# Score matmuls of the first head pair: from 64 contracted rows to 128, through query tiles padded with zeros

## The chip, the cores and the metric

One Trainium2 chip, one core of it. The time is device microseconds (us) of one execution; lower is better. The kernel before takes 513.86 us, the median of three runs that lie between 513.81 and 513.95 us.

## The reference, cut to what matters

The program is attention, then a feed-forward network, then a mixture of experts. The change lies in the attention scores; what follows uses them.

```python
B, H, S, D = q.shape                       # 2, 8, 576, 64
scores = scale * np.matmul(q, k.transpose(0, 1, 3, 2))
mask = block_i >= block_j                  # blocks of 64 positions
scores = np.where(mask, scores, -1000000000.0)
scores = scores - np.max(scores, axis=-1, keepdims=True)
attn = np.exp(scores)
attn = attn / (np.sum(attn, axis=-1, keepdims=True) + 1e-09)
return np.matmul(attn, v)
...
x = attn_out, tokens by model width: 1152 x 512
h = x @ w_in; g = elu(h); x = g @ w_out    # feed-forward, 2048 wide
...                                        # router to 8 experts, two layers each, scaled by the gate
```

## The kernel before, in words

Sixteen heads (two batches of eight) are worked on as eight pairs of heads; a pair is called m, its heads a and b. `part1` does the attention, `part2` the feed-forward network and the router, `part3` the experts. On all five engines of `part1` the order of the work is the program's own, written out by hand in the string `ORDER` (lines 26 to 34): each word is a step, the letter a or b is the head, the last digit says how many rounds behind the round i the step's pair is. A round is one pass through `ORDER`.

The steps that matter here:

- `K` (`turn`, line 358) transposes a pair's keys or queries on TensorE, 128 positions at a time, so that the 64 head dimensions of head a lie in rows 0 to 63 and those of head b in rows 64 to 127. `k` then splits the result in a high part (ScalarE, line 375) and a low part, the rest (VectorE, line 376). Keys and queries are each done in two groups g, of 256 and 320 positions.
- `S` (`scores`, line 396) multiplies queries by keys into PSUM. A head's 576 queries are five tiles t (one of 64 and four of 128), handled in three parts; a piece is one tile against at most 512 keys. The first tile of a round's scores is `S20`. Each piece has one bank in PSUM, and the next head's piece may only start when the exponentials of the one before it have been read out.
- A product in full precision is high*high + high*low + low*high. For the pairs 1 to 7 the queries' high and low parts are stacked in one tile of 128 rows (`stack`, line 342, four DMAs on SP's queue) and the keys' high part is doubled (`double`, line 331, on GpSimd), so that two matmuls of 128 rows do the work: `kk` against `qq`, and the keys' low part `kl`, with zeros in the other head's rows (`lows`, line 352), against `qq`. Pair 0 is not stacked: it takes three matmuls per piece of 64 rows each, on the rows of the head (line 411). Its output has `nq` rows (line 406), which is 64 for the first tile.
- The last 64 columns of a tile's scores are masked by a small matmul of 128 rows (line 425).
- `M` takes the row maxima on VectorE (line 436), `E` the exponentials on ScalarE (line 449), `D` sums and reciprocals on VectorE, `N` the normalization on GpSimd (line 476), `T` the transposes of the probabilities on TensorE (lines 495, 499 and 520), `V` the product with the values (line 536).

Before round 0 the program fills constants. VectorE's memsets come first: `kr` and `qr` (line 554), then `mrow` and `mcol` (lines 562 to 564). GpSimd fills the larger tiles meanwhile (lines 566 to 578). TensorE runs 42 small matmuls on `mrow` (line 581), transposes pair 0's keys and queries (lines 582 to 585), and runs four more small matmuls (line 588). Twelve more stand ahead of the eighth to the nineteenth of the steps `S`, `T` and `K` (line 643).

Of the kernel before, what the change touches and what calls it, by code (L numbers as in the profile page):

```python
# [9 lines left out]
FP32 = mybir.dt.float32  # L10
F32R = mybir.dt.float32r
# [3 lines left out]
ACTF = mybir.ActivationFunctionType  # L15
ALU = mybir.AluOpType
# [26 lines left out]
def attention_ffn_moe(  # L43
# [13 lines left out]
    nc = tc.nc  # L57
    B, H, S, D = q.shape
# [216 lines left out]
    def part1():  # L275
# [5 lines left out]
        xx_p = p1.enter_context(tc.tile_pool(name="xx", side="left", bufs=2))  # L281
# [15 lines left out]
        qraw, kraw, vt, qT, kT, prob, stat = {}, {}, {}, {}, {}, {}, {}  # L297
# [6 lines left out]
        )  # L304
        PROB = [[at.tile([128, 640], FP32, name=f"prob{part}{i}") for i in range(2)] for part in range(3)]

        KLO = [xx_p.tile([128, 2, S], F32R, name=f"kl{i}", bufs=1) for i in range(2)]

        def load(m, src, ring, queue=nc.sync):
# [42 lines left out]
        def lows(m):  # L352

            for h in range(2):
                own = slice(64 * h, 64 * h + 64)
                nc.sync.dma_start(out=KLO[m % 2][own, h].bitcast(FP32), in_=kT[m][1][own].bitcast(FP32))

        def turn(m, which, g, pool=ps_t, tag="t"):

            src, dst, sc = (qraw, qT, SCALE) if which == "q" else (kraw, kT, 1.0)  # L360
            if g == 0:
                dst[m] = tuple(qt_p.tile([128, S], F32R, tag=which + x, name=which + x) for x in "hl")
            js = range(NK)[2 * g:2 + (NK - 2) * g]
            a, e = 128 * js[0], min(S, 128 * (js[-1] + 1))
            bank = pool.tile([128, 512], FP32, tag=tag, name="qkT")
            ps = bank[:, 0:e - a]
            for j in reversed(js):
                nc.tensor.transpose(
                    out=bank[:, 128 * j - a:128 * j - a + 128],
                    in_=src[m][:, j].rearrange("r h d -> r (h d)"),  # L370
                    identity=ident,
                )
            hv, lv = (x[:, a:e] for x in dst[m])
            return [
                lambda: nc.scalar.activation(out=hv, in_=ps, func=ACTF.Copy, scale=sc),
                lambda: nc.vector.scalar_tensor_tensor(
                    out=lv, in0=ps, scalar=sc, in1=hv.bitcast(FP32), op0=ALU.mult, op1=ALU.subtract
                ),
            ]


        parts = [[(4, 0)], [(3, 0), (0, 448)], [(2, 0), (1, 320)]]
# [1 line left out]
        def split(t):  # L384

            nk = sum(QT[t])
            nb = (nk + 511) // 512
            return nb, nk // nb
# [7 lines left out]
        def scores(n, part, i):  # L396

            m, h = divmod(n, 2)
            r0 = 64 * h
            t, b, c0, k0, w = PIECES[part][i]  # L400
            if c0 == 0:
                banks[n, part, b] = ps_s.tile([128, 512], FP32, tag=f"s{part}{b}", name="s")
            bank, (q0, nq) = banks[n, part, b], QT[t]
            rows = slice(r0, r0 + 64)

            wq = 128 if m else nq
            if m:
                xq = stacked[m, "q"][:, h]
                todo = [(xq, stacked[m, "k"][:, h]), (xq, KLO[m % 2][:, h])]
            else:  # L410
                todo = [(qT[m][x][rows], kT[m][z][rows]) for x, z in ((0, 0), (0, 1), (1, 0))]
            end = t > 0 and k0 + w == q0 + nq
            for y, (x, z) in enumerate(todo):
                nc.tensor.matmul(
                    out=bank[0:wq, c0:c0 + w],
                    lhsT=x[:, q0:q0 + wq],
                    rhs=z[:, k0:k0 + w],
                    start=(y == 0 and (part != 2 or c0 == 0)),
                    stop=(y == len(todo) - 1 and not end),
                    skip_group_check=(part == 2),  # L420
                )

            def mask():
                if end:
                    nc.tensor.matmul(  # L425
                        out=bank[:, c0 + w - 64:c0 + w],
                        lhsT=mrow, rhs=mcol, start=False, stop=True,
                        skip_group_check=(part == 2),
                    )

            return mask
# [130 lines left out]
        nc.vector.memset(mrow, 0.0)  # L562
        nc.vector.memset(mrow[:, 0:64], 1.0)
        nc.vector.memset(mcol, -1e8)
        stats = [[st_p.tile([128, 8], FP32, name=f"stat{i}{j}") for j in range(3)] for i in range(3)]
        for x in stats:
            nc.gpsimd.memset(x[1], 1.0)
# [3 lines left out]
        for x in VT:  # L571
            nc.gpsimd.memset(x[64:128, NK - 1], 0.0)
        for x in KLO:
            for h in range(2):
# [7 lines left out]
        for w in "kq":  # L582
            for g in range(2):
                for f in turn(0, w, g, ps_s, ("s10", "s20", "s00", "s01")[2 * "kq".index(w) + g]):
                    f()
# [32 lines left out]
        def do(name, h, m):  # L618
# [25 lines left out]
            if kind == "S":  # L644
                pend[n, name] = scores(n, *rest)
                if name == "S21":
                    pend[n, "S20"]()
                if name != "S20":
                    pend[n, name]()
            elif kind == "M":  # L650
                largest_of_two(n, 4) if rest == [0, 2] else largest(n, *rest)
            elif kind == "E":
                power(n, *rest)
            elif kind == "D":
                if rest == [0, 0]:
                    total_of_two(n, 4)
                elif rest[1] == (1 if rest[0] == 0 else 0):
                    total(n, rest[0])
                else:
                    inverse(n, rest[0])  # L660
            elif kind == "N":
                norm(n, *rest)
            elif kind == "T":
                pend[n, name] = turn_ends(n) if name == "TE" else turn_p(n, rest[0])
            elif kind == "t":
                pend[n, name[:2].upper()][rest[-1]]()
            elif kind == "K":
                if m + 1 < NM:
                    pend[n, name] = turn(m + 1, "kq"[h], rest[0])
            elif kind == "k":  # L670
                if m + 1 < NM:
                    pend[n, name[:2].upper()][rest[1]]()
# [629 lines left out]
    with tc.manual_schedule(engines=every):  # L1302
        part1()
# [31 lines left out]
```

## Time and profile before

| what | value |
|---|---|
| median of the runs | 513.86 us (513.81 to 513.95) |
| the profiled execution | 514.5 us, its span from first to last instruction 512.8 us |
| TensorE (PE) busy | 487.3 us, 95% of the span, 2842 matmuls |
| VectorE (DVE) busy | 341.3 us, 67% |
| ScalarE (ACT) busy | 311.7 us, 61% |
| GpSimd (POOL) busy | 118.0 us, 23% |
| mean granted TensorE clock | 0.976 of full speed |

The profile is one execution on the chip. PE is TensorE's matmuls, PEld its weight loads, which run beside them; SPq, ACTq and the like are the engines' queues, which issue DMAs. A clock of 1.00 is TensorE's upper level, 2.4 GHz; 0.50 is the lower, 1.2 GHz. Times in the rows are us from the span's start, durations us unless marked ns. A matmul's end is modelled, so durations of neighbours overlap; the distance between two starts is the better measure of what a matmul costs in a stream. The stretches:

| us from the start | what runs |
|---|---|
| 0 to 9.6 | constants, pair 0's keys and queries |
| 9.6 to 24.3 | pair 0's scores, both heads |
| 24.3 to about 112 | the remaining pairs, a round of some 11.7 us each |
| about 112 to 440 | feed-forward network, router, first experts |
| 440 to 512.8 | last experts |

### The profile page before, as it was taken

How to read it: one execution, taken by the hardware profiler on the slowest of the kernel's cores; microseconds unless marked ns; L12 is line 12 of the kernel's file. 1: busy time of each engine (PE TensorE's matmuls, PEld its weight loads, DVE VectorE, ACT ScalarE, POOL GpSimd, SP SyncE). 2: the span in 40 equal slices, each digit the busy share in tenths (PEclk: the TensorE clock that was granted, in tenths of full speed). 3: DMA queues.
4: the chain of work that ended last, by engine and by line, in shares of the span. 5: the costliest groups of instructions: out<-in, count | busy, mean ns of one | idle time of the engine just before them, and what ended most of it. 6: DMA issues, size and time to landing. Idle time of an engine off the chain costs nothing. (4 is left out here: it accounts for less than half of the span.)

```text
span 512.8 us, 8712 instructions
## 1 busy us (share of the span) xinstructions
PE 487.3 (95%) x2842; PEld 403.3 (79%) x2842; DVE 341.3 (67%) x828; ACT 311.7 (61%) x699; POOL 118.0 (23%) x219
## 2 busy tenths in 40 slices
PE   7999999999999999999999999989898889999994
PEld 6678888879997889999998888767676768786683
DVE  4489898969977999994464365564467965461451
ACT  4478899867865666753554455373567875552551
POOL 6266878650000000000000022311121330100211
PEclk9599999999999999999999999999999989999998
DMA  8758775503689985340131043269389886280100
GB/s 195 164 140 197 186 167 133 153 15 117 185 249 228 281 272 159 97 138 12 35 91 42 1 143 124 67 242 336 117 324 345 296 273 267 80 317 20 42 33 24
DMA packets 61254, 80.86 MB, mean 158 GB/s; under 512 B 33170, under 2 KB 33170, under 8 KB 61200
## 3 DMA queue, kind: packets, MB, share of 16 engines
q1 hardware_dynamic: 58368, 75.18, 48.4%
q0 software_dynamic: 1632, 4.72, 2.5%
q8 instruction: 28, 0.46, 0.4%
q10 hardware_dynamic: 1200, 0.30, 0.3%
q14 instruction: 26, 0.21, 0.1%
HBM read 62.17 MB, written 12.41 MB: 145 GB/s over the span
## 5 line engine op out<-in xcount | busy, mean ns | idle before, releaser
L260 PE MATMUL acc<-wbh,gh 128*128 128x512 f32 x144 | 57.3, 398 | 0.0
L260 PE MATMUL acc<-wbh,gl 128*128 128x512 f32 x144 | 57.2, 397 | 0.0
L260 PE MATMUL acc<-wbl,gh 128*128 128x512 f32 x144 | 57.1, 397 | 0.0
L904 POOL DMA_INDIRECT disp<-y_all,slot x9 | 9.1, 1016 | 201.7 <-DVE e L245 179.0
L87 DVE TENSOR_TENSOR xl<-rb,xh 128x1024 fp32r<-128x1024 f32 (+1 forms) x36 | 38.9, 1100 | 22.2 <-ACT xh L1116 19.0
L476 POOL TENSOR_SCALAR prob<-prob,stat 128x576 f32<-128x576 f32 (+3 forms) x80 | 42.3, 542 | 32.5 <-DVE stat L470 19.4
L449 ACT ACTIVATE prob<-s,stat 128x288 f32<-128x288 f32 (+4 forms) x96 | 45.4, 480 | 2.4 <-DVE stat L464 1.1
L243 ACT ACTIVATE e<-h 128x384 f32<-128x384 f32 x48 | 23.3, 484 | 36.4 <-PE h L233 34.0
L186 DVE SCALAR_TENSOR_TENSOR cv_t<-r,cv_t 128x512 int32<-128x512 int32 x64 | 44.1, 690 | 0.3
L87 DVE TENSOR_TENSOR xl<-ra,xh 128x1024 fp32r<-128x1024 f32 (+1 forms) x36 | 39.3, 1101 | 7.0 <-ACT xh L1116 6.1
L233 PE MATMUL h<-xh,wah 128*128 128x384 f32 x192 | 42.3, 341 | 1.6 <-DVE e L245 1.4
L436 DVE TENSOR_REDUCE stat<-s 128x1 f32<-128x288 f32 (+4 forms) x96 | 37.8, 423 | 6.5 <-PE s L425 4.3
L233 PE MATMUL h<-xl,wah 128*128 128x384 f32 x192 | 41.6, 337 | 0.0
L233 PE MATMUL h<-xh,wal 128*128 128x384 f32 x192 | 41.1, 336 | 0.0
L245 DVE SCALAR_TENSOR_TENSOR e<-e,h 128x384 f32<-128x384 f32 x48 | 26.4, 550 | 21.2 <-ACT e L244 21.0
L233 PEld LDWEIGHTS h<-xh,wah 128*128 128x128 f32 x192 | 34.2, 188 | 6.8 <-DVE e L245 2.9
L1216 PE MATMUL acc<-xh,gh 128*128 128x512 f32 (+1 forms) x96 | 39.3, 410 | 0.0
L1216 PE MATMUL acc<-xh,gl 128*128 128x512 f32 (+1 forms) x96 | 38.0, 395 | 0.0
L1216 PE MATMUL acc<-xl,gh 128*128 128x512 f32 (+1 forms) x96 | 37.8, 394 | 0.0
L1243 POOL DMA_INDIRECT out<-o,gt x12 | 11.7, 972 | 112.0 <-ACTq L1290 34.6
L1116 ACT ACTIVATE xh<-ra 128x1024 fp32r<-128x1024 f32 (+1 forms) x36 | 34.3, 961 | 5.0 <-PE h L233 2.8
L249 ACT ACTIVATE gh<-e 128x384 fp32r<-128x384 f32 x48 | 25.1, 522 | 16.7 <-DVE e L245 16.1
(171 smaller groups left out, 1178.5 us busy)
## 6 DMA issues: line engine op xcount, KB each, us to landing
ra<-in_moe_w SPq DMA_DIRECT2D x32, 512.0 KB, 6.1
rb<-in_moe_w SPq DMA_DIRECT2D x32, 512.0 KB, 7.9
r<-in_moe_w_in SPq DMA_DIRECT2D x16, 512.0 KB, 6.4
r<-in_moe_w_out SPq DMA_DIRECT2D x16, 512.0 KB, 4.4
disp<-z SPq DMA_DIRECT2D x18, 257.0 KB, 6.9
rows<-disp SPq DMA_DIRECT2D x14, 257.0 KB, 4.3
out<-z SPq DMA_DIRECT2D x9, 256.0 KB, 4.0
kr<-in_k SPq DMA_DIRECT2D x16, 128.0 KB, 2.9
```

What stands on the lines that cost most here:

```text
L87: eng.tensor_tensor(out=lo, in0=x, in1=hi.bitcast(FP32), op=ALU.subtract)
L186: nc.vector.scalar_tensor_tensor(out=st["t"], in0=x(), scalar=scalar, in1=st["t"], op0=op, op1=ALU.bitwise_or)
L233: nc.tensor.matmul(out=h[:, f, :], lhsT=w[:, kk, (f0 + f) * 128:(f0 + f + 1) * 128], rhs=x[:, kk, t0:t0 + n], start=(i == 0), stop=(i == l ...
L243: nc.scalar.activation(out=e, in_=hf, func=ACTF.Relu, scale=-1.0)
L245: nc.vector.scalar_tensor_tensor(out=e, in0=e, scalar=-1.0, in1=hf, op0=ALU.add, op1=ALU.max)
L249: nc.scalar.activation(out=gh, in_=ef, func=ACTF.Copy)
L260: nc.tensor.matmul(out=acc[t], lhsT=x[:, f, t * 128:(t + 1) * 128], rhs=w[:, f0 + f, :], start=(first and f == 0 and i == 0), stop=(last a ...
L436: nc.vector.tensor_reduce(out=stat[n][0][0:nq, t + b:t + b + 1], in_=banks[n, part, b][0:nq, c0:c0 + w], axis=AX.X, op=ALU.max, negate=True,)
L449: nc.scalar.activation(out=prob[n, part][0:nq, c0 + k0:c0 + k0 + w], in_=banks[n, part, b][0:nq, c0:c0 + w], func=ACTF.Exp, bias=stat[n][0 ...
L476: nc.gpsimd.tensor_scalar(out=p, in0=p, scalar1=stat[n][2][0:nq, t:t + 1], scalar2=0.0, op0=ALU.mult, op1=ALU.add)
L1116: lambda: nc.scalar.activation(out=hi, in_=r, func=ACTF.Copy),
L1216: nc.tensor.matmul(out=acc[0:n], lhsT=x[:, f % 4, 0:n], rhs=y[:, f % 2, :], start=(f == 0 and i == 0), stop=(f == NF - 1 and i == 2),)
```

## The change

Two tiles `QZ` of 128 rows, 2 heads and 576 positions are added, one for the high and one for the low part of pair 0's scaled queries. Each head's slot holds that head's 64 rows and zeros in the other 64; four memsets on VectorE write the zeros, placed behind all its other constants. Pair 0's queries are split from PSUM into these tiles, a head at a time, so that each of the two groups takes two ScalarE and two VectorE instructions on 64 rows where it took one and one on 128. Pair 0's score matmuls then contract 128 rows: the padded queries against the keys of both heads. Their number stays three per piece. The output of the first tile's piece takes 128 rows in place of 64.

```diff
+        QZ = [xx_p.tile([128, 2, S], F32R, name=f"qz{i}", bufs=1) for i in range(2)]
...
-            hv, lv = (x[:, a:e] for x in dst[m])
-            return [
-                lambda: nc.scalar.activation(out=hv, in_=ps, func=ACTF.Copy, scale=sc),
-                lambda: nc.vector.scalar_tensor_tensor(
-                    out=lv, in0=ps, scalar=sc, in1=hv.bitcast(FP32), op0=ALU.mult, op1=ALU.subtract
-                ),
-            ]
+            def split(hv, lv, x):
+                return [
+                    lambda: nc.scalar.activation(out=hv, in_=x, func=ACTF.Copy, scale=sc),
+                    lambda: nc.vector.scalar_tensor_tensor(
+                        out=lv, in0=x, scalar=sc, in1=hv.bitcast(FP32), op0=ALU.mult, op1=ALU.subtract
+                    ),
+                ]
+            if m == 0 and which == "q":
+                res = []
+                for h in range(2):
+                    own = slice(64 * h, 64 * h + 64)
+                    res.append(split(*(x[own, h, a:e] for x in QZ), ps[own]))
+                return [f for fs in zip(*res) for f in fs]
+            return split(*(x[:, a:e] for x in dst[m]), ps)
...
-            wq = 128 if m else nq
+            wq = 128
...
-                todo = [(qT[m][x][rows], kT[m][z][rows]) for x, z in ((0, 0), (0, 1), (1, 0))]
+                todo = [(QZ[x][:, h], kT[m][z]) for x, z in ((0, 0), (0, 1), (1, 0))]
...
         nc.vector.memset(mcol, -1e8)
+        for x in QZ:
+            for h in range(2):
+                nc.vector.memset(x[64 - 64 * h:128 - 64 * h, h].bitcast(FP32), 0.0)
```

## Rows read from the trace of the kernel before

**Rows 1.** Windows by stage: length, busy us (instructions) per engine, clock, DMA share, GB/s

```profile
9.60:13.30 3.70, 3.70 (x24) 2.82 (x23) 2.39 (x7) 2.07 (x6) 2.13 (x4) 1.00 1.03 234
13.30:25.10 11.80, 11.45 (x50) 7.79 (x49) 4.95 (x21) 5.57 (x22) 3.15 (x6) 0.50 0.71 158
...
37.40:49.10 11.70, 11.70 (x107) 9.43 (x106) 10.47 (x41) 10.42 (x37) 8.09 (x14) 1.00 0.80 197
```

**Rows 2.** Windows of 0.2 us, PE alone: length, busy us, clock, DMA share, GB/s

```profile
13.20:13.40 0.20, 0.20 (x3) 0.85 0.28 63
...
26.80:27.00 0.20, 0.20 (x2) 0.52 0.73 229
```

**Rows 3.** Timeline of PE, rounds 0 and 1: start, us, instruction, idle before it

```profile
17.07 0.74 PE L414 MATMUL s<-kh,qh 64*128 64x448 f32 x1
...
21.69 0.23 PE L425 MATMUL s<-mcol,mrow 128*128 128x64 bf16 x1
...
24.34 0.45 PE L495 MATMUL pT<-ident,prob 128*128 128x128 f32 x1 [0.19 <-DVE stat L470]
...
25.08 0.62 PE L414 MATMUL s<-kk,qq 128*128 128x320 f32 x1
...
27.37 0.66 PE L520 MATMUL pE<-ident,prob 128*128 128x128 f32 x4
```

**Rows 4.** Waits of PE from 36 to 442 us, the longest single one: total us, times, longest

```profile
PE hx L1195 <- DVE dl L87: 2.3, 1, 2.3
```

**Rows 5.** Windows of 2 us among the experts, PE alone: length, busy us, clock, DMA share, GB/s

```profile
402.00:404.00 2.00, 0.94 (x7) 1.00 0.93 278
...
416.00:418.00 2.00, 2.00 (x6) 0.53 0.34 68
```

**Rows 6.** Timeline of DVE: its first memsets, and the splits of pairs 0 and 1

```profile
0.91 0.30 DVE L554 MEMSET kr<- 64x128 f32 x2 [0.91 <-PEq L1320]
...
7.28 0.87 DVE L376 SCALAR_TENSOR_TENSOR kl<-qkT,kh 128x256 fp32r<-128x256 f32 x2 [5.35 <-ACT kh L375]
8.07 0.81 DVE L376 SCALAR_TENSOR_TENSOR ql<-qkT,qh 128x256 fp32r<-128x256 f32 x2
8.80 0.81 DVE L376 SCALAR_TENSOR_TENSOR kl<-qkT,kh 128x256 fp32r<-128x256 f32 x2
```

**Rows 7.** Timeline of PE ahead of the first scores

```profile
9.27 0.44 PE L368 MATMUL qkT<-ident,qr 128*128 128x128 f32 x2 [0.79 <-DVE kl L376]
```

**Rows 8.** Timeline of PE: scores of pair 0, head a

```profile
9.63 0.41 PE L414 MATMUL s<-kh,qh 64*128 64x320 f32 x1
...
11.55 0.20 PE L425 MATMUL s<-mcol,mrow 128*128 128x64 bf16 x1
...
11.68 0.24 PE L414 MATMUL s<-kh,qh 64*64 64x64 f32 x1
...
13.57 0.29 PE L643 MATMUL warm<-mrow 128*128 128x128 bf16 x1
```

**Rows 9.** Timeline of PE: in round 2, the steps of 24.34 to 27.37 us

```profile
37.39 0.27 PE L495 MATMUL pT<-ident,prob 128*128 128x128 f32 x1
...
38.88 0.20 PE L425 MATMUL s<-mcol,mrow 128*128 128x64 bf16 x1
38.92 0.28 PE L414 MATMUL s<-kk,qq 128*128 128x64 f32 x1
...
39.15 0.66 PE L520 MATMUL pE<-ident,prob 128*128 128x128 f32 x4
```

**Rows 10.** Timeline of ACT: the split and exponentials ahead of head b's second part

```profile
14.54 0.44 ACT L375 ACTIVATE qh<-qkT 128x320 fp32r<-128x320 f32 x1 [1.79 <-PE qkT L368]
...
15.77 0.49 ACT L449 ACTIVATE prob<-s,stat 128x288 f32<-128x288 f32 x1
```

**Rows 11.** SP's queue: head a's second stacking DMA; median us to landing of such

```profile
15.56 0.54 SPq L348 DMA_DIRECT2D qq<-ql x1
...
qq<-ql SPq DMA_DIRECT2D x14, 144.0 KB, 2.5
```

More of the change, by code (lines that the diff above doesn't have):

```diff
@@ L398, in scores @@
             m, h = divmod(n, 2)
-            r0 = 64 * h
             t, b, c0, k0, w = PIECES[part][i]
@@ L403, in scores @@
             bank, (q0, nq) = banks[n, part, b], QT[t]
-            rows = slice(r0, r0 + 64)
-            wq = 128 if m else nq
+            wq = 128
             if m:
```

## The prediction

> **What bounds the kernel now.** TensorE is busy for 95% of the span, so I look for stretches where it works below its pace. I read the windows by stage first. From 9.6 to 13.3 us PE works without a gap at the upper clock; from 13.3 to 25.1 us it is still busy for 11.45 of 11.80 us, but the granted clock is 0.50, the 1.2 GHz level; in round 2 it is at 1.00 again and never idle [rows 1]. The small windows put the fall between 13.2 and 13.4 us and the return at 27.0 us [rows 2]. The timeline says what PE did before each. Ahead of the fall it had run 64-row score matmuls since 9.63 us, with 128-row work only in short masks and warming matmuls between [rows 8]. The clock stayed low through head b, also 64 rows. At 24.34 us 128-row transposes start, at 25.08 us the first 128-row scores, and 1.9 us after those the clock is back [rows 3]. All through the low stretch VectorE (4.95 of 11.80 us) and ScalarE (5.57) have room [rows 1], so there PE sets the pace.
>
> Where time won here ends up: from round 2 PE is the bound, 11.70 busy us in 11.70 [rows 1], and the order of work is fixed, so a round that begins earlier moves everything behind it. Later waits of PE are on engines that move along with it; the longest single one, 2.3 us on VectorE [rows 4], is between two stages of the same chain. I expect a gain at round 2 to reach the end whole, but for the clock among the experts (below).
>
> **The change, part by part.** *Memsets.* Four on VectorE, each 64x576. The nearest row is `kr`: two of 64x128 in 0.30 us, 0.15 us each [rows 6]. Scaled by 576/128 that is 0.68 us each, 2.7 us in all; by count alone 0.6 us. I take the upper end. VectorE sits idle for 5.35 us before its first split at 7.28 us [rows 6], and the memsets stand behind `mrow`, on which PE's warming matmuls wait, so they cost nothing; if they took over 5.35 us, what is over would delay the splits.
>
> *The split by heads.* Each of the two query groups takes two VectorE instructions where it took one, so two more. Two of 128 rows took 0.73 us from start to start (8.07 to 8.80) [rows 6]. For 64 rows the same length bounds it above, half of that below, 0.37 us more; with as many elements per row I take the same length: +0.73, say 0.8. Behind it stands pair 1's key split, for whose buffer PE waits 0.79 us before the transposes at 9.27 us [rows 7]; so the first score starts at 10.4 us in place of 9.63. ScalarE's two more instructions run beside these.
>
> *Head a's scores.* The number and the columns of the matmuls stay; wider output of the first tile adds nothing to the columns. What goes is the change between 64-row and 128-row matmuls at every mask and warming matmul. From a mask to the next score it is 0.13 us with 64-row scores (11.55 to 11.68) [rows 8] and 0.04 us where both have 128 rows (38.88 to 38.92) [rows 9]: 0.09 us for a change. From 9.63 to 13.57 us there are nine of them: -0.8 us. The bounds are 0 and 1.0. So head a ends where it did, at 13.57 us.
>
> *The clock, head b.* With 128-row scores I expect no fall. From 13.57 to 17.07 us PE does three transposes and head b's first part at the lower clock; half of 3.50 us is 1.75, which puts the second part at 15.3 us. Its bank is free only when ScalarE has split pair 1's queries and read out head a's first two exponentials of that part, 1.23 us (14.54 to 15.77) [rows 10], from about 14.05 us, so also at 15.3: no further gain there. From 17.07 us [rows 3] to the last mask at 21.69 is 4.62 us, half of it 2.31; seven row changes less take off 0.6 (0 to 0.6): 17.0 us. From that mask to 24.34 us VectorE's maxima and splits set the pace, 2.65 us; I take 2.5 us (between 2.3, the part without waits on PE, and 2.65). The transposes of round 1 then start at 19.5 us in place of 24.34: 4.8 us earlier.
>
> *Round 1 up to 27.37 us.* The stretch takes 3.03 us, mostly at the lower clock [rows 3]; the same steps in round 2 take 1.76 us (37.39 to 39.15) [rows 9]. That is 1.27 us more, if GpSimd's normalization keeps up; 0 if it does not.
>
> *Queues.* SP's stacking DMAs for pair 1 wait on the same split and move little. Head a's second is issued at 15.56 us and such a one lands 2.5 us later [rows 11], 18.1 us, ahead of the 19.9 us at which it is now wanted: covered by 1.8 us. Behind them SP only issues loads, which are wanted a round later. The unused query tile of pair 0 costs nothing.
>
> **Sum:** +0.8 - 0.8 - 1.8 - 2.9 - 0.1 - 1.3 = -6.1 us. The profiled execution took 514.5 us with a span of 512.8 us, 0.6 us over the median; the difference is taken off the median: 513.86 - 6.1 = **507.8 us**. Bounds of this case: without the row changes of head b, the 0.15 us and the last term, a gain of 4.1 us, 509.8 us. On the other side round 1 still holds PE idle time: PE was never idle in round 2 [rows 1], and if round 1 came to the same, some 1 us more is won, 506.8 us.
>
> One thing moves either way. Among the experts PE has gaps, and not all are followed by the same clock: at 402 us, where PE is busy for only 0.94 of 2 us, it stays at 1.00, while at 416 us it is at 0.53 over two busy us [rows 5]. Which of them cost the clock may differ once everything lies 6 us earlier. A stretch like that costs about 1.5 us, won or lost; I take none.
>
> **The rivals.** *A, forecast:* no fall, 506.8 to 509.8 us, likeliest 507.8.
>
> *B, a short fall.* PE's gap before the first scores doubles, from 0.79 to about 1.6 us, and the clock falls there, ahead of the first score; 128-row scores then bring it back. The nearest rows are 1.9 us from the first such scores to the return, and 3.7 us of scores before the fall [rows 2, 3, 8]. At half pace that gives back 0.9 to 1.9 us: 508.7 to 509.7, or 511 with A's lower bound. Against it: the clock stayed up at 402 us [rows 5].
>
> *C, rows are not the cause.* The clock falls and returns as before, because it hangs on something that the padding leaves alone. The Trainium skill, "TensorE: Matmul & The Clock Gate", Part 1, says that the gate follows how busy TensorE has recently been, with no word of how many rows a matmul fills; by that the padding would leave the clock as it is. What is left in this case is +0.8 for the splits, -0.8 and -0.6 for the row changes: 513.3 us, between 512.5 (splits free) and 514.7 (no row changes gained). Against it speaks the row in which PE is busy for 11.45 of 11.80 us at the lower clock [rows 1]: that page's rule alone does not explain it, and what differs on its two sides is the rows. For it: the zeros may count as little as the missing rows did. But the later pairs' `kl` has zeros in half its rows too, and their clock is 1.00.
>
> *D, slower.* The doubled gap lowers the clock before the first score, and rows of zeros do not bring it back until round 1. Head a's 3.1 us then take 6.2: its end moves from 13.57 to 16.6 us, +3.0, less 0.6 for head b: 516.3 us. It decides once the gap over 0.79 us is enough for a fall; without a fall ahead of the scores there is no way to such a loss.
>
> **How the numbers follow.** A 0.70, B 0.12, C 0.10, D 0.08. The time is A's. Its own range is 506.8 to 509.8; B's reaches to 511. The range goes from 506.4, which allows for a part of a low stretch among the experts that is won, to B's 511.0 us; C and D, 0.18, lie outside. About 0.2%, 1.0 us, is what a measurement of this kernel can tell from no change. A and B are faster: 0.82. C is within it: 0.10. D is slower: 0.08.
>
> **What would show it.** Right: a granted clock of 1.00 from 9.6 to 27 us, the first score near 10.4 us, head b's second part waiting shortly for ScalarE near 15.3 us, round 1's transposes near 19.5 us, round 2's near 31.3 us, rounds of 11.7 us after. A clock of 0.50 from about 13.3 us with 128-row matmuls shows C, one that is low from about 10 us B or D, told apart by its return. First scores still at 9.6 us would prove the split's term wrong; a gain at round 2 that is not there at the end would prove the passing on wrong.

## The result, and the profile after

The changed kernel took 507.33 us, the median of 12 runs, against 513.78 us for the kernel before in 12 runs beside them: a ratio of 0.989, 95% interval 0.987 to 0.991. Forecast were 507.8 us and a range of 506.4 to 511.0. The single runs lie between 505.8 and 512.3 us, before between 511.2 and 515.5: both kernels vary by several us, more than the three runs shown ahead of the prediction suggested. Line numbers shift by up to 12 in the changed kernel.

The windows by stage of the changed kernel, to be read against [rows 1] (columns as there):

```profile
9.60:13.30 3.70, 3.21 (x25) 2.83 (x25) 2.82 (x8) 1.97 (x6) 2.46 (x4) 1.00 1.09 249
13.30:25.10 11.80, 10.24 (x86) 8.62 (x85) 9.24 (x39) 9.26 (x35) 5.92 (x12) 1.00 0.71 159
25.10:27.00 1.90, 1.90 (x17) 1.59 (x15) 1.90 (x7) 1.20 (x5) 1.77 (x3) 1.00 0.90 301
37.40:49.10 11.70, 11.70 (x107) 9.45 (x106) 10.98 (x45) 10.56 (x38) 8.32 (x15) 1.00 0.87 216
```

From 13.3 to 25.1 us the clock is at 1.00 in place of 0.50, and PE gets through 86 matmuls in place of 50. The low stretch is gone, and the later rounds are unchanged, 11.70 us busy in 11.70.

The timeline of PE shows where the stages begin, to be read against [rows 3, 8 and 9]:

```profile
5.80 0.72 PE L370 MATMUL qkT<-ident,kr 128*128 128x128 f32 x5
...
7.13 0.71 PE L370 MATMUL qkT<-ident,kr 128*128 128x128 f32 x5
10.09 0.44 PE L370 MATMUL qkT<-ident,qr 128*128 128x128 f32 x2 [2.25 <-DVE kl L379]
10.29 0.39 PE L423 MATMUL s<-kh,qz 128*128 128x320 f32 x1
...
13.36 0.22 PE L655 MATMUL warm<-mrow 128*128 128x128 bf16 x1
...
15.33 0.48 PE L423 MATMUL s<-kh,qz 128*128 128x448 f32 x1 [0.29 <-ACT prob L458]
...
17.53 0.20 PE L434 MATMUL s<-mcol,mrow 128*128 128x64 bf16 x1
...
19.72 0.30 PE L504 MATMUL pT<-ident,prob 128*128 128x128 f32 x1 [0.25 <-DVE stat L479]
...
21.50 0.66 PE L529 MATMUL pE<-ident,prob 128*128 128x128 f32 x4
...
31.57 0.27 PE L504 MATMUL pT<-ident,prob 128*128 128x128 f32 x1
```

Round 2 begins at 31.57 us where it began at 37.39, 5.8 us earlier. The first score begins 0.7 us later (10.29 against 9.63), behind a wait for VectorE that has grown from 0.79 to 2.25 us [rows 7]. This although the first transposes start at 5.80 us here and at 6.37 us in the profile of before; over the profiles of this study, with the same front of the program or not, that start lies between 5.78 and 6.37 us, so it is chance.

The feed-forward network's first accumulation then starts at 114.18 us against 120.02, again 5.8 us earlier. The span is 504.7 us against 512.8, 8.1 us less; the other 2.3 us come from later places that differ between executions of the same program (last section).

### The profile page after: what moved, and what is told of

Read it like the earlier page. It is cut to its first block, busy times and chain, and to the rows that moved or that the text cites. A ratio compares the mean times of both kernels' runs of the same rounds, so it can differ in the third digit from the quotient of the medians.

```text
span 504.7 us, 8722 instructions
## 1 busy us (share of the span) xinstructions
PE 479.9 (95%) x2842; PEld 400.2 (79%) x2842; DVE 344.2 (68%) x834; ACT 311.9 (62%) x701; POOL 118.9 (24%) x219
## 5 line engine op out<-in xcount | busy, mean ns | idle before, releaser
L249 ACT ACTIVATE gh<-e 128x384 fp32r<-128x384 f32 x48 | 25.1, 523 | 16.6 <-DVE e L245 16.0
```

Of the source, the lines that this page charges most:

```text
L249: nc.scalar.activation(out=gh, in_=ef, func=ACTF.Copy)
```

## The experiments

Because the end varies, I compare by marks in round 0 to 2, which the order of work fixes. All are us from the start of one profiled execution; "low" is the stretch at a clock of 0.50. "First transposes" are those of pair 0's keys, "pair 1's keys" the last group of transposes ahead of PE's wait for VectorE.

| kernel | first transposes | pair 1's keys | first score | low | head b's second part | round 1 | round 2 |
|---|---|---|---|---|---|---|---|
| before | 6.37 | 7.76 | 9.63 | 13.3 to 27.0 | 17.07 | 24.34 | 37.39 |
| changed | 5.80 | 7.13 | 10.29 | none | 15.33 | 19.72 | 31.57 |
| changed, again (e8) | 6.37 | 8.46 | 11.65 | 11.3 to 14.8 | 18.13 | 22.50 | 34.35 |
| changed, third (e12) | 6.37 | 8.11 | 11.27 | none | 16.31 | 20.68 | 32.54 |
| e1, own 64 rows | 6.36 | 8.04 | 11.38 | 13.9 to 31.0 | 19.87 | 27.46 | 40.85 |
| e2, before with 128 rows | 6.37 | 8.27 | 9.95 | none | 14.84 | 19.04 | 30.91 |
| e3, head a on 64 | 5.91 | 7.23 | 10.56 | 12.2 to 19.0 | 18.87 | 23.31 | 35.16 |
| e4, no warming | 5.84 | 7.16 | 10.32 | none | 15.17 | 19.32 | 31.20 |
| e5, memsets twice | 5.78 | 7.10 | 10.72 | 11.9 to 15.3 | 17.34 | 21.71 | 33.58 |
| e6, head b's split later | 5.89 | 7.22 | 8.91 | none | 14.34 | 18.72 | 30.58 |
| e7, e6 without warming | 6.37 | 7.70 | 9.39 | none | 14.67 | 18.84 | 30.69 |
| e9, e6 again | 6.15 | 7.47 | 9.17 | none | 14.60 | 18.96 | 30.83 |
| e10, e7 again | 6.00 | 7.32 | 9.02 | none | 14.30 | 18.48 | 30.34 |
| e11, gap filled | 6.36 | 8.23 | 11.39 | none | 16.44 | 20.83 | 32.68 |

The times ahead of pair 1's keys vary by over 1 us, with the change and without it, so what the change itself does is best read from that mark on. The row of before, to be read beside 7.13 and 10.29 us above:

```profile
7.76 0.72 PE L368 MATMUL qkT<-ident,kr 128*128 128x128 f32 x5
```

From there to round 2 it is 29.63 us in the kernel before, 24.44 and 24.43 us in the first and third profile of the changed one, 25.89 us in e8: the change itself wins 5.2 us up to round 2, or 3.7 us in e8, and the rest of the 5.8 us above is an earlier start.

My theory was the forecast's: 64-row scores let the clock fall, 128-row scores hold it. The rivals were that something else in the change holds it, and that the warming matmuls are needed besides.

### e1: everything of the change but the rows

```diff
-                todo = [(QZ[x][:, h], kT[m][z]) for x, z in ((0, 0), (0, 1), (1, 0))]
+                own = slice(64 * h, 64 * h + 64)
+                todo = [(QZ[x][own, h], kT[m][z][own]) for x, z in ((0, 0), (0, 1), (1, 0))]
```

> The changed kernel with its padded tiles, memsets and split by heads, but the score matmuls of pair 0 read only the head's own 64 rows again. If the number of contracted rows is what the clock hangs on: first score at about 10.3 us as in the changed kernel, the clock falls to 0.50 between 13 and 15 us and stays there to about 27 us, round 2's first transpose (31.57 us in the changed kernel, 37.39 before) comes at 38 to 39 us. If the clock hangs on something else that the change moved, such as when the scores start: clock 1.00 throughout, round 2 at 31.5 to 32.5 us.

One execution took 516.73 us, the kernel before beside it 512.67. The clock fell as expected, here in windows of PE alone (length, busy us, clock, DMA share, GB/s):

```profile
13.80:14.00 0.20, 0.20 (x3) 0.82 0.96 230
14.00:14.20 0.20, 0.20 (x2) 0.50 0.91 207
14.20:29.80 15.60, 15.25 (x61) 0.50 0.61 149
...
30.80:31.00 0.20, 0.20 (x2) 0.52 0.06 23
31.00:31.20 0.20, 0.20 (x4) 1.00 0.06 23
```

PE is busy for 15.25 of 15.60 us and the clock stays low all the same. That puts the cause in the rows of the scores: memsets, padded tiles and the split by heads are those of the changed kernel, and with 64 rows contracted the low stretch is back, 17 us long. In the eleven profiles in which both heads' scores have 128 rows no low stretch up to round 2 is longer than 3.6 us. What the runs do not separate is the number of rows from the steady change between 64-row scores and 128-row masks and warming matmuls, which goes with it in before, in e1 and in head a of e3. The forecast of round 2, 38 to 39 us, was too early: it came at 40.85, as the first score was 1.1 us later than I said and the clock came back 2.8 us after round 1's first scores (28.20 us), not 1.9.

### e2: nothing of the change but the rows

```diff
-                todo = [(qT[m][x][rows], kT[m][z][rows]) for x, z in ((0, 0), (0, 1), (1, 0))]
+                todo = [(qT[m][x], kT[m][z]) for x, z in ((0, 0), (0, 1), (1, 0))]
```

> The kernel before, with pair 0's score matmuls over all 128 rows of the unsplit, unpadded queries and keys: the scores of pair 0's two heads are summed, which leaves out their separation, and no memset and no split by heads is added. If rows are the cause, the clock stays at 1.00, the first score starts at 9.6 us as before, and round 2 comes 0.5 to 0.8 us ahead of the changed kernel's 31.57 us, so near 30.9 us; the difference of the first scores, 0.66 us, is then the price of the split. If the zeros or the split are needed for the gain, the clock falls at 13 us and round 2 stays at 37 us.

One execution took 507.61 us. The clock is at 1.00 throughout, and round 2 comes at 30.91 us, as forecast for the rows alone. So neither zeros nor split are needed to hold the clock; they are there for the scores' sake, and cost time. The first score of e2 starts 1.68 us behind the transposes of pair 1's keys (8.27 to 9.95), that of the changed kernel 3.16 us (7.13 to 10.29, and 8.11 to 11.27 in its third profile): between two kernels with 128-row scores the split costs 1.5 us, and against the kernel before (1.87 us) 1.3.

A new wait shows too. Timeline of PE at the start of round 2 in e2:

```profile
30.91 0.27 PE L495 MATMUL pT<-ident,prob 128*128 128x128 f32 x1
31.02 0.49 PE L499 MATMUL pT<-ident,prob 128*128 128x128 f32 x3
32.34 0.38 PE L414 MATMUL s<-kk,qq 128*128 128x320 f32 x1 [0.84 <-ACT pt L486]
```

Pair 2's first scores wait 0.84 us. The profile names ScalarE, but its work may not be what was late: these matmuls read pair 2's stacked queries, whose DMAs took 6.6 to 6.9 us to land in this stretch, issued from 24.66 and 25.30 us on (2.5 us is the median of before [rows 11]), so they landed shortly ahead of 32.34 us; in e10, below, the profile names the DMA.

### e3: head a on 64 rows, head b on 128

```diff
-                todo = [(QZ[x][:, h], kT[m][z]) for x, z in ((0, 0), (0, 1), (1, 0))]
+                own = slice(0, 64) if h == 0 else slice(0, 128)
+                todo = [(QZ[x][own, h], kT[m][z][own]) for x, z in ((0, 0), (0, 1), (1, 0))]
```

> The changed kernel with head a of pair 0 on 64 rows and head b on 128. If 64-row scores let the clock fall and 128-row scores bring it back: a fall between 13 and 15 us, a return within 2 to 4 us of 128-row scores, at 17 to 20 us, and round 2 at 32.5 to 34.5 us. If a clock that has fallen stays low until round 1 whatever the rows of head b: return near 26 us, round 2 at 36 to 38 us. If head b's rows alone had mattered: no fall, round 2 near 32.2 us (head a's row changes cost 0.8 us).

One execution took 511.11 us. The clock fell at 12.2 us and came back with head b, whose 128-row scores began at 16.90 us:

```profile
12.20:18.80 6.60, 6.60 (x29) 0.50 0.43 99
18.80:19.00 0.20, 0.20 (x5) 0.50 0.95 207
19.00:19.20 0.20, 0.20 (x3) 0.89 0.97 207
```

The return, 2.1 us after the first of them, is inside the 2 to 4 us of the theory, and far from the 26 us of its rival. So 128-row scores with zeros in half their rows do not only hold the clock, they bring it back. Round 2 at 35.16 us is 0.7 us later than my range; the fall came earlier than I assumed. Whether head a's rows or the gap ahead of them caused this particular fall, this run does not say.

### e4: without the warming matmuls

```diff
-KEEP_WARM = range(8, 20)
+KEEP_WARM = range(0)
```

> The changed kernel without the twelve warming matmuls between the steps of rounds 0 and 1. If 128-row scores hold the clock by themselves: clock 1.00 from 9.6 to 27 us, and round 2 at 31.2 to 31.6 us, since the twelve take some 0.04 us each and PE waits for ScalarE and VectorE in that stretch anyway. If the warming matmuls are still needed: a fall between 13 and 20 us and round 2 at 33 us or later.

One execution took 508.80 us. The clock is at 1.00 from 9.6 to 31 us; round 2 comes at 31.20, 0.4 us earlier than the changed kernel's 31.57 for nearly the same start. The padded scores held the clock without them here.

### e5: the memsets twice

```diff
-        for x in QZ:
+        for x in QZ * 2:
             for h in range(2):
                 nc.vector.memset(x[64 - 64 * h:128 - 64 * h, h].bitcast(FP32), 0.0)
```

> The changed kernel with its four memsets run twice. The eight take 0.695 us each from start to start and end near 7.65 us; VectorE's first split starts at 6.65 to 7.45 us in the runs so far. If the four cost nothing because VectorE waits for the transposes anyway, the doubled set delays the first split to 7.65 us and no later, and the first score by 0.2 to 1.0 us; the warming matmuls start at 1.91 us as before. If memsets on VectorE already delayed the splits, the second set adds its whole 2.8 us: first score near 13 us.

One execution took 511.18 us, beside 514.47 for the kernel before. The timeline of VectorE, and PE's gap:

```profile
7.03 0.54 DVE L576 MEMSET qz<- 64x576 f32 x1 [0.16 <-issue]
7.49 0.75 DVE L379 SCALAR_TENSOR_TENSOR kl<-qkT,kh 128x256 fp32r<-128x256 f32 x2
...
10.53 0.44 PE L370 MATMUL qkT<-ident,qr 128*128 128x128 f32 x2 [2.71 <-DVE kl L379]
```

The first split starts at 7.49 us, as the last memset ends, 0.84 us later than in the changed kernel (6.65), and the first score 0.43 us later. So four memsets do hide in VectorE's idle time, and what runs over delays the scores, as the forecast had it. What I had not expected is the clock: it fell behind the gap, to 0.50 from 11.9 to 15.3 us, with 128-row scores on both sides, and came back while they ran. This is the short fall of rival B, only that it began 1.2 us behind the first score and not ahead of it. Round 2 was 2.0 us later than in the changed kernel.

### e6 and e7: head b's split later, and without warming

```diff
-                return [f for fs in zip(*res) for f in fs]
+                put_off.append(res[1])
+                return res[0]
...
                     do(x, h, i - d)
+                    if i == 0 and (x, h) in (("k00", 1), ("M20", 0)):
+                        for fs in put_off:
+                            fs.pop(0)()
```

> The changed kernel, in which head b's half of the query split (two ScalarE and two VectorE instructions) is issued behind pair 1's key split and first query split, head a's half where it was. If the split by heads is what delays the first score, the distance from VectorE's first split to the first score falls from 3.6 to 3.9 us to about 2.4 us, as in the kernel before (2.35), clock 1.00, and round 2 comes at 30.6 to 31.2 us. If the delay has another cause, or the instructions moved only delay head a's maxima and exponentials instead: round 2 at 31.3 us or later.

> The same with the twelve warming matmuls taken out too. If both gains hold and add up: clock 1.00, round 2 at 30.2 to 30.8 us, 0.4 us ahead of the kernel with only the split moved. If what the warming matmuls took is hidden by waits for ScalarE once the scores begin earlier: the same round 2 within 0.1 us.

One execution each took 508.96 and 508.36 us. VectorE and PE in e6:

```profile
6.74 0.87 DVE L380 SCALAR_TENSOR_TENSOR kl<-qkT,kh 128x256 fp32r<-128x256 f32 x2 [2.02 <-ACT kh L379]
7.53 0.81 DVE L380 SCALAR_TENSOR_TENSOR qz<-qkT,qz 64x256 fp32r<-64x256 f32 x2
8.26 0.80 DVE L380 SCALAR_TENSOR_TENSOR kl<-qkT,kh 128x256 fp32r<-128x256 f32 x2
...
8.72 0.44 PE L371 MATMUL qkT<-ident,qr 128*128 128x128 f32 x2 [0.78 <-DVE kl L380]
```

From VectorE's first split to the first score it is 2.17 us (6.74 to 8.91), in the changed kernel 3.64 (6.65 to 10.29), in the kernel before 2.35: the split of the second head is the delay. PE's gap is back at 0.78 us. Round 2 comes at 30.58 us, 1.0 us earlier. Without the warming matmuls it comes at 30.69 with a start 0.5 us later, so another 0.4 us is won up to there.

### e8, e9 and e10: does it reach the end?

e8 is the changed kernel, e9 is e6, e10 is e7, timed on one chip in pairs with the kernel before.

> The changed kernel itself, timed in pairs with the kernel before: 506 to 510 us against 512 to 515 us, a ratio near 0.988. Rounds 0 to 2 of its profile: if the 2.25 us gap of PE before the first scores is safely short for the clock, clock 1.00 from 9.6 to 31 us and round 2 at 31.5 to 32.1 us as before. If it is short enough only in some executions, which the doubled memsets' 2.71 us gap suggests, this profile or a part of the timed runs shows a fall of some 3.4 us near 12 us and 1.6 us more, and the times spread over more than 2 us.

> The kernel with head b's query split issued later, its gap before the first scores being 0.78 us as in the kernel before: round 2 at 30.6 to 31.1 us, 1.0 us ahead of the changed kernel. If that reaches the end: 1 us faster than the changed kernel in the same call, about 506 us. If what follows takes it back (the weights' loads, the clock among the experts): the same as the changed kernel within 1 us.

> The same without the twelve warming matmuls: round 2 another 0.2 to 0.5 us earlier for the same start of the first transposes; the end 0 to 0.5 us earlier. If the warming matmuls hold the clock in some executions: a wider spread than the kernel with them, and a slower median.

| kernel | median us | lowest to highest | ratio to before, 95% interval |
|---|---|---|---|
| before | 515.37 | 513.8 to 515.9 | |
| e8, changed | 510.08 | 508.65 to 513.23 | 0.9897 [0.9875, 0.9919] |
| e9, split later | 509.22 | 507.54 to 510.19 | 0.9875 [0.9853, 0.9896] |
| e10, and no warming | 509.00 | 508.77 to 510.27 | 0.9887 [0.9867, 0.9906] |

In the profile of e8, of the changed kernel itself, the clock falls short and early:

```profile
11.20:11.40 0.20, 0.08 (x1) 0.89 1.14 255
11.40:11.60 0.20, 0.20 (x2) 0.50 1.10 245
11.60:14.40 2.80, 2.80 (x13) 0.50 0.76 177
...
14.60:14.80 0.20, 0.20 (x3) 0.58 0.88 196
14.80:34.30 19.50, 17.42 (x147) 1.00 0.70 167
```

Round 2 comes at 34.35 us in place of 31.57 and 32.54 in the other two profiles; of that 1.5 us are the fall (25.89 us from pair 1's keys on, against 24.44), the rest is a later start. Rival B is thus not a rival of the forecast but part of it: some executions of the changed kernel have the short fall. In e6, e7, e9 and e10, with a gap of 0.8 us, none of four profiles has it.

The 0.9 to 1.1 us by which e9 and e10 lie below e8 are within the intervals, so whether they beat the changed kernel stays open. Part of what the earlier first score won is given back. PE at round 2 of e10:

```profile
30.34 0.27 PE L506 MATMUL pT<-ident,prob 128*128 128x128 f32 x1
...
31.32 0.38 PE L425 MATMUL s<-kk,qq 128*128 128x320 f32 x1 [0.39 <-DMA qq<-ql]
```

Pair 2's stacked queries are now what is late; in e9 the same wait (0.33 us) comes a round later. The feed-forward network starts at 114.29 us in e9 and 114.11 in e10, where the changed kernel has 114.18 in its first profile and 115.18 in its third.

### e11 and e12: the gap filled

```diff
+                    if m == 0 and h == 1 and rest[0] == 0:
+                        for _ in range(38):
+                            nc.tensor.matmul(out=warm[:, 0:128], lhsT=mrow, rhs=mrow, start=True, stop=True)
                     pend[n, name] = turn(m + 1, "kq"[h], rest[0])
```

> The changed kernel with 38 more warming matmuls ahead of pair 1's first query transposes, where PE otherwise waits 2.15 to 2.25 us for VectorE; at 0.053 us each they take 2.0 us. If that gap is what lets the clock fall near 12 us in some executions, this profile shows a gap under 0.5 us and clock 1.00 from 9.6 to 31 us, the first score comes where the wait for VectorE puts it anyway, and the timed runs lie closer together and 0.5 to 1.5 us below the changed kernel's of the same call. If the fall has another cause, it shows in as many executions as before and the times are the same.

> The changed kernel once more, for a third profile and for comparison with the filled gap on the same chip: ratio near 0.989. Where its profile has the clock at 1.00 through round 0, round 2 comes at 31.5 to 32.2 us; where the clock falls near 12 us, at 33.5 to 34.5 us.

Timeline of PE in e11: the warming matmuls stand where it waited, and the transposes still come when VectorE is ready.

```profile
8.23 0.72 PE L370 MATMUL qkT<-ident,kr 128*128 128x128 f32 x5
8.78 2.29 PE L683 MATMUL warm<-mrow 128*128 128x128 bf16 x38
11.20 0.44 PE L370 MATMUL qkT<-ident,qr 128*128 128x128 f32 x2
```

e11 took 506.94 us in the median (506.31 to 508.52), ratio 0.9876 [0.9853, 0.9899]; e12, the changed kernel on the same chip, 507.77 us (506.92 to 509.29), ratio 0.9897 [0.9875, 0.9919]; before 513.47. Neither profile has a fall in round 0, so this pair does not show the gap to be the cause; from pair 1's keys to round 2 it is 24.45 us in e11 and 24.43 in e12, so that the filling itself neither costs nor wins anything there. The filled kernel's median is 0.8 us lower and its runs hardly closer together, and the intervals overlap. What stands is a count: with a gap of 2.15 to 2.71 us and 128-row scores after it, two profiles of five (changed three times, e4, e5) have the short fall; with 0.8 us or a filled gap, none of six (e2, e6, e7, e9, e10, e11). That the gap does it fits this, and is not proved by it.

## Why the prediction was right, and where it was wrong

**The main step held.** The clock stayed up because of the rows: without the rows the whole change brings nothing (e1), the rows alone bring all of it (e2). The Trainium skill's rule in "TensorE: Matmul & The Clock Gate", Part 1, that the gate follows how busy TensorE was, would have given rival C. That rule alone does not fit these rows: from 13.3 to 25.1 us PE was busy for 11.45 of 11.80 us at 0.50 before and for 10.24 of 11.80 us at 1.00 after, and in e1 for 15.25 of 15.60 us at the lower level. Here the measurement goes beyond the page.

**Term by term**, in the profile of the changed kernel, each stage's length against that of before:

| term | forecast | measured |
|---|---|---|
| split by heads, ahead of the first score | +0.8 | +1.3 (1.87 to 3.16, from pair 1's keys) |
| head a's row changes | -0.8 | -0.9 (3.94 to 3.07) |
| to head b's second part | -1.8 | -1.5 (3.50 to 1.97) |
| head b's second part to its last mask | -2.9 (2.3 clock, 0.6 row changes) | -2.4 (4.62 to 2.20) |
| to round 1's transposes | -0.1 | -0.5 (2.65 to 2.19) |
| round 1 to its fourth transposes | -1.3 | -1.3 (3.03 to 1.78) |
| sum | -6.1 | -5.2 |

From the first score to round 2 the kernel before needs 27.76 us and the changed one 21.28 in the first profile and 21.27 in the third; forecast were 6.9 us less, measured 6.5. In head b's second part the clock's share came as forecast and the row changes hardly did (half of 4.62 is 2.31 us, measured 2.20); the shorter way to round 1's transposes made up for that. *Memsets:* forecast 0.68 us each, measured 0.70 from start to start (0.54 busy and 0.16 issue), hidden as said. *Wider output of the first tile*, put at nothing: its three matmuls take 0.34 us in the changed kernel (11.93 to 12.27), 0.18 us in e2 (11.59 to 11.77), where the output stays at 64 rows, so 0.16 us a head; it stands within the two score terms of the table.

**The term that was mis-sized is the split**, +1.3 us in place of +0.8, above all by its price of 0.37 us for a VectorE instruction of 64 rows ("with as many elements per row I take the same length"). ScalarE and VectorE of the changed kernel:

```profile
6.23 0.76 ACT L378 ACTIVATE kh<-qkT 128x256 fp32r<-128x256 f32 x2 [2.28 <-PE qkT L370]
6.89 1.67 ACT L378 ACTIVATE qz<-qkT 64x256 fp32r<-64x256 f32 x4
8.58 0.71 ACT L378 ACTIVATE kh<-qkT 128x256 fp32r<-128x256 f32 x2
...
7.68 1.90 DVE L379 SCALAR_TENSOR_TENSOR qz<-qkT,qz 64x256 fp32r<-64x256 f32 x4 [0.16 <-ACT qz L378]
9.61 0.82 DVE L379 SCALAR_TENSOR_TENSOR kl<-qkT,kh 128x256 fp32r<-128x256 f32 x2
```

ScalarE in the kernel before:

```profile
7.52 0.71 ACT L375 ACTIVATE qh<-qkT 128x256 fp32r<-128x256 f32 x2
8.18 0.76 ACT L375 ACTIVATE kh<-qkT 128x256 fp32r<-128x256 f32 x2
```

The four on VectorE take 1.93 us from the first to the next one's start (7.68 to 9.61), 0.48 each, where the two of before took 0.73, 0.37 each [rows 6]: 1.20 us more. The four on ScalarE take 1.69 us, 0.42 each, where a pair of 128-row ones takes 0.66 (7.52 to 8.18), 0.33 each. That "ScalarE's two more instructions run beside these" held but for 0.24 us: VectorE's first low part starts 1.03 us behind its first split (6.65 to 7.68), 0.79 us before (7.28 to 8.07), and the profile puts 0.16 us of that on ScalarE. From the last transposes to the first score 0.16 us is won (0.36 to 0.20, 128-row scores behind 128-row transposes). Together these give the 1.3 us.

Measured from the first transposes, the first profile shows 1.2 us and the third 1.6 us more than before. Of the third's, 0.35 us lies ahead of the split: pair 0's transposes took longer there (6.37 to 8.11 us, before 6.37 to 7.76), and so they did in e2, which has no split (6.37 to 8.27). So the first score came near the forecast's 10.4 us, at 10.29, only because that execution began early; that is luck. Up to round 2 the terms came to 5.2 us where 6.1 were forecast.

**Rival B was given too little, 0.12.** I set the longer gap at 1.6 us; it is 2.2, and one of three profiles of the changed kernel has the fall. By the prediction's own terms its upper end is 509.8 + 1.9 = 511.7 us, not 511. The row that I brought against it, the clock that stayed up at 402 us, stands behind 128-row matmuls of the experts, not behind transposes and warming matmuls: too far from the case. Its price, 0.9 to 1.9 us, is right for the clock: from the first score to round 2 e8 takes 22.70 us against 21.28, 1.4 us more.

**The passing on** held up to the feed-forward network in two of the three profiles: 5.84 us there after 5.82 at round 2 in the first, 4.84 after 4.85 in the third. In e8 it did not, 2.14 us (117.88 us) after 3.04; there PE waits 0.64 us for pair 6's stacked queries at 82.26 us. Beyond, the end moved by what no step foresaw, and in both directions. That the median came out 6.45 us lower than before, where the change itself won 5.2 us by round 2, or 3.7 with the short fall, is therefore probably in part scatter of the later stages. The medians of the two later sets of runs differ by less, 5.3 us (e8) and 5.7 us (e12): that the forecast's point was hit to 0.5 us is luck.

## What to carry to other kernels

Where PE is nearly always busy and the granted clock is low, look at what it runs, not at how much: matmuls over half of the contracted rows did not keep the clock here, and zeros in the other half did. Before splitting an instruction by heads, look whether ScalarE and VectorE both feed the next step of the chain, and whether the second half is wanted that early; e6 took 1.5 us out of that chain by asking for it later. A gap on PE just ahead of the work that the clock is to be kept for is a risk of its own, and shows only in some executions: take more than one profile.

## What the runs showed of the hardware

*A clock that rows of zeros hold.* With padded scores in both heads, half of whose products are with zeros, TensorE stayed at 2.4 GHz up to round 2 in eight of ten profiles; the other two (e5, e8) had the short fall. Where the clock was at 1.2 GHz it came back 2.1 us (e3) and 3.1 us (e8) behind the first of such scores.

*Instructions on alternating halves.* ScalarE's 64-row instructions cost 0.33 us each from start to start where two of one head follow each other (e6: 6.98 to 7.64 us for the pair) and 0.42 where the two heads alternate; VectorE's 0.37 (e6: 7.53 to 8.26 us) and 0.48. 128-row ones cost 0.33 and 0.37 in the kernel before, so fewer rows made nothing cheaper. Why the alternation costs more was not tried.

*Scatter behind the change.* In the profile of before PE waited 1.2 us at 164 us for VectorE, which waited behind ScalarE for a load of weights; in the changed one it waited 0.2 us. The low clock among the experts at 416 us is gone in the changed profile; at the router it is longer:

```profile
324.00:326.00 2.00, 2.00 (x10) 0.50 0.10 37
326.00:328.00 2.00, 2.00 (x10) 0.50 0.59 226
...
334.00:336.00 2.00, 2.00 (x6) 0.50 1.02 406
```

The kernel before has one such stretch there, near 332 us, and e11 none. None of these stands in a fixed relation to the change. The wait is worth 1.2 us; a low stretch is worth at most half its length, by estimate 1.8 us for the 3.5 us at 416 us, and up to 5.5 us for the 11 us at the router of the changed profile.
